# Placing the low parts of H by time in a routed expert kernel: set times, four H banks, a refitted placing model

## The chip, the cores and the metric

The kernel runs on one core of a Trainium2 chip. The metric is the device time of one execution in microseconds (us); smaller is better. The engines are PE (matrix products, with a queue of weight loads beside it), DVE (vector arithmetic), ACT (activations and copies), POOL (here it issues the gathers and scatters) and SP (plain DMA issues).

## The reference, cut to what matters

A batch of 8 sequences (512 local and 32 global tokens, 8 heads of 64) goes through windowed attention; its output is x, N = 8 x 544 = 4352 tokens by 512. Then E = 8 experts, each with room for N // E = 544 tokens, are filled greedily from the largest gate value down:

```python
cap = N // E
logits = x @ w_gate
order = np.argsort(-logits.flatten())
for idx in order:                      # largest first
    tok, e = idx // E, idx % E
    if assigned[tok] >= 0 or counts[e] >= cap: continue
    assigned[tok] = e; counts[e] += 1
for e in range(E):
    mask = assigned == e
    h = np.maximum(x[mask] @ w1[e], 0.0)   # 512 -> 1024
    out[mask] = h @ w2[e]                  # 1024 -> 512
```

## The kernel before

The attention fills the first part of the span (to about 240 us); the change does not touch it. Then `experts` runs eight experts one after the other, numbered from 0 here. Beside each expert's products, the *routing* finds the tokens of the next one: eight search steps (matmuls `r_oh,r_G` and `r_ce,big` on PE, a scan and comparisons on DVE), then which expert was filled (`vs`, `widx`: which weights to gather), a prefix sum (`r_cs`), one-hot tables (`r_ohh`, `rhs`, four pieces `r_ohl`), the matmuls `r_ohl,rhs` and `c,r_w` on PE, and from these the token list `idx`, by which POOL gathers x.

An expert's products are made in fp32r with a high and a low part of each operand, so that three products (high-high, high-low, low-high) stand for one in full precision:

- *H stage*: 16 blocks H, each 128 rows of h by 272 tokens, 12 matmuls a block (line 876 before). ACT writes the high part `hh` as Relu of the PSUM bank, DVE then the low part `hl` = max(H, 0) - hh; after that the bank is free.
- a small product for the last 32 tokens (line 893), in full precision out of `h32`.
- *Y stage*: four tiles Y of 128 tokens by 512, 24 matmuls each (line 903); ACT copies each to `y`, POOL scatters it to the output. "Y40" is the place behind the 40th of these 96 matmuls.

Between them lie, for the *next* expert: the gather of its W1 (`w1r`, two of 1 MB) and W2 (`w2r`), the split of both into high (ACT, `w1h`, `w2h`) and low parts (DVE, `w1l`, `w2l`), the gather of its x (`xg`, five tiles), their transposes on PE into H banks (line 741), and the split into `xh` (ACT) and `xl` (DVE).

All instructions of an engine run in the order in which the program was written, and this order is set by a placing model while the program is built. `V.now` is the model's time on PE: each matmul adds a constant (`step`). `V.busy` is when DVE would be through with all it has been given: each operation adds a fixed charge and a charge per element (`Queue`). Work for later is kept in a list `todo` with a time and a condition; `step` starts at most one such piece per matmul when its time has come. Where the condition has `calm()`, DVE must be less than AHEAD = 200 ns behind. The routing is a generator: it yields the model time from which it may go on (`ready`: DVE's end + 400 ns; `pace`: DVE's end - 250 ns). Before, it yields -1 where an `hl` may go in: `bubble` then issues what is in `fill`. `bubble` is also called when DVE would be idle, and at the end of a block all that is in `fill` is issued ahead of adding the new one. At an expert's end a loop lets the model's time run on, with no matmul, until the next expert's gathers, W1's first half and the transposes have been placed:

```python
while nxt < E and (pending(f"g{nxt}", f"h{nxt}", f"a{nxt}", f"x{nxt}", f"v{nxt}") or nxt not in raw1):
    step(120)
    bubble()
```

PSUM's eight banks are H 3, Y 3 and two for the routing (R, R2).

Of the kernel before, what the change touches and what calls it, by code (L numbers as in the profile page):

```python
# [8 lines left out]
F32 = mybir.dt.float32  # L9
# [4 lines left out]
ALU = mybir.AluOpType  # L14
# [4 lines left out]
B, H, SL, SG, D = 8, 8, 512, 32, 64  # L19
S = SL + SG  # L20
DM = H * D
# [351 lines left out]
HOP = 400  # L373
SLACK = 100
PACE = 250
CU = 64
LAND = 1000
CF = 1024
# [4 lines left out]
class Queue:  # L383
# [12 lines left out]
    def __getattr__(s, name):  # L396
        op = getattr(s.eng, name)

        def issue(*args, **kw):
            aps = [x for x in list(args) + list(kw.values()) if hasattr(x, "dtype") and hasattr(x, "shape")]  # L400
            n = max(int(np.prod(x.shape[1:])) for x in aps)
            fast = name in ("tensor_scalar", "tensor_copy") or name == "tensor_tensor" and all(
                mybir.dt.size(x.dtype) == 2 for x in aps)
            s.busy = max(s.busy, s.now) + 130 + n * (2.2 if "scan" in name else 0.55 if fast else 1.05)
            return op(*args, **kw)  # L405
        return issue


class Routing:
# [103 lines left out]
    def search(s):  # L513
        nc = s.nc
        for it in range(NIT):
            yield -1
            yield s.when
            A = s.ps.tile([128, 2, E], F32, name="R")
            for i in range(18):
                j, r = slice(2 * i, 2 * i + 2), 32 * (i % 4)  # L520
                g, o = (s.G[:, j].rearrange("p a b -> p (a b)"), s.oh[:, j]) if i < 17 else (s.one, s.rem)
                s.mm(A[r:r + 32], g, o, ns=20, start=(i < 4), stop=(i >= 14))
            p = s.ps.tile([128, 16, E], F32, name="R2")
            if it == 0:
                lo = s.t("lo", [34], I32)
                lof = s.t("lof", [34])
                s.V.tensor_scalar(lo, s.u, 0xffff, None, op0=ALU.bitwise_and)
                s.V.tensor_scalar(lof, lo, 2.0 ** -16, None, op0=ALU.mult)
                s.x = s.hi
            else:  # L530
                x = s.t("x%d" % (it % 2), [34])
                if it == 3:
                    s.V.scalar_tensor_tensor(x, s.x, P, lof, op0=ALU.subtract, op1=ALU.add)
                else:
                    s.V.tensor_scalar(x, s.x, P, None, op0=ALU.subtract)
                s.x = x
            ce = s.t("ce", [2, 16, E], F16)
            s.V.tensor_tensor(ce, A[:, :, None, :].to_broadcast([128, 2, 16, E]),
                              s.dk[:, :, :, None].to_broadcast([128, 2, 16, E]), op=ALU.mult)
            when = s.V.ready()  # L540
            yield -1
            yield when
            for k in range(2):
                s.mm(p, s.big, ce[:, k], start=(k == 0), stop=(k == 1))
            pm = s.t("pm%d" % (it % 2), [16 * E])
            s.V.tensor_tensor_scan(pm, p.rearrange("p a b -> p (a b)"), s.fin[:, it], 0.0, op0=ALU.max,
                                         op1=ALU.min)
            P = pm[:, 16 * E - 1:16 * E]
            if it < NIT - 1:
                s.cand(s.x, P, it + 1)  # L550
        s.P = P.bitcast(I32)

    def phase(s, ph):
# [16 lines left out]
        a = s.t("a", [34])  # L570
# [18 lines left out]
        p = s.ps.tile([128, 68], F32, name="R")  # L589
# [4 lines left out]
        if more:  # L594
            g = s.t("gt", [34], BF16)
# [12 lines left out]
        hl = s.t("hl", [2, 34], I32)  # L608
# [10 lines left out]
        rhs = s.rhs  # L619
# [3 lines left out]
        ohl = s.t("ohl", [64, 34], BF16)  # L623
        for k in range(4):
            q = slice(16 * k, 16 * k + 16)
# [10 lines left out]
        p = s.ps.tile([128, 64], F32, name="R2")  # L636
        for j in range(34):
            r = 32 * (j % 4)
            s.mm(p[r:r + 32], rhs[:, :, :, j].rearrange("p a b -> p (a b)"), ohl[:, :, j], ns=20, start=(j < 4),
                 stop=(j >= 30))  # L640
        if not last:
            s.V.scalar_tensor_tensor(s.act, s.wt, vs, s.act, op0=ALU.not_equal, op1=ALU.mult)
        if more:
# [3 lines left out]
                                     op1=ALU.min)  # L647
# [8 lines left out]
        p = s.ps.tile([128, 6], F32, name="R2")  # L656
# [26 lines left out]
def experts(ctx, tc, A, xd, ident, rt, out):  # L683
# [3 lines left out]
    ps = ctx.enter_context(tc.tile_pool(name="fps", bufs=1, space=PSUM))  # L687
# [7 lines left out]
    hh = wp.tile([128, 8, CAP], F32R, name="hh")  # L695
    hl = wp.tile([128, 8, CAP], F32R, name="hl")
    h32 = wp.tile([128, 8, 32], F32, name="h32")
    sizes = [128, 128, 128, 128, 32]
    HF = CAP // 2
# [36 lines left out]

    def trans_x(xg, t):
        n = sizes[t]
        p = ps.tile([128, 4, 128], F32, name="H", bufs=3)
        for d in range(4):  # L740
            nc.tensor.transpose(p[:, d, :n], xg[t][:n, 128 * d:128 * d + 128], ident[:n, :n])  # L741
        q = slice(128 * t, 128 * t + n)
        nc.scalar.activation(xh[:, :, q], p[:, :, :n], AF.Copy)
        V.tensor_tensor(xl[:, :, q], p[:, :, :n], xh[:, :, q], op=ALU.subtract)
# [12 lines left out]
    V = rt.V  # L757
    V.now = V.busy = 0.0
    pool, dma, need = [0.0], [0.0], [0.0]
    fill, todo, raw1 = [], [], {}  # L760
# [17 lines left out]

    routing = chain()

    def bubble():
        while fill:
            fill.pop(0)()

    def at(tag, t, f, cond=None):
        todo.append((tag, t, cond, f))
# [8 lines left out]

    def step(ns):
        V.now += ns
        for i, (tag, t, cond, f) in enumerate(todo):
            if t <= V.now and (cond is None or cond()):
                todo.pop(i)  # L800
                f()
                break
        while not done[0] and V.now >= need[0]:
            v = next(routing, None)
            if v is None:
                done[0] = True
            elif v < 0:
                bubble()
            else:
                need[0] = v  # L810
        if V.busy < V.now and (done[0] or need[0] > V.now + SLACK):
            bubble()

    def low1(p, j):
        split_w1(raw1[p], j, V)
# [40 lines left out]
    def ffn(ph):  # L856
        nxt = ph + 1
        t0 = V.now
        cur[0] = ph
        half = []  # L860
        if nxt < E:
            at(f"g{nxt}", t0, lambda: get_w1(nxt, half), lambda: nxt in rt.widx and not pending(f"b{ph}"))
            at(f"h{nxt}", t0, lambda: get_x(nxt), lambda: nxt in rt.idx and (mid[0] == ph or V.now > t0 + TX))
            at(f"v{nxt}", t0, lambda: get_w2(nxt), lambda: mid[0] == ph and nxt in rt.widx and
               (not pending(f"h{nxt}") or V.now > t0 + TW))
        for f in range(8):
            if f == 4:
                force(f"b{ph}")
                half.append(True)
            for hf in range(2):  # L870
                q = slice(HF * hf, HF * hf + HF)
                p = ps.tile([128, HF], F32, name="H", bufs=3)
                fs = slice(128 * f, 128 * f + 128)
                for d in range(4):
                    for k, (w, x) in enumerate(((w1h, xh), (w1h, xl), (w1l, xh))):
                        nc.tensor.matmul(p, w[d][:, fs], x[:, d, q], start=(d + k == 0), stop=(d + k == 5))  # L876
                        step(117)
                nc.scalar.activation(hh[:, f, q], p, AF.Relu)  # L878
                if hf:
                    nc.scalar.activation(h32[:, f], p[:, HF - 32:HF], AF.Relu)  # L880
                while fill:
                    fill.pop(0)()
                fill.append(lambda p=p, f=f, q=q: V.scalar_tensor_tensor(
                    hl[:, f, q], p, 0.0, hh[:, f, q], op0=ALU.max, op1=ALU.subtract))

        while fill:
            fill.pop(0)()
        force(f"w{ph}")

        p = ps.tile([128, 128], F32, name="Y", bufs=3)  # L890
        for f in range(8):
            for c in range(4):
                nc.tensor.matmul(p[32 * c:32 * c + 32], h32[:, f], w2r[f // 4][:, f % 4, 128 * c:128 * c + 128],  # L893
                                 start=(f == 0), stop=(f == 7))
            step(220)
        mid[0] = ph
        out_tile(ph, 4, p)
        for t in range(4):
            p = ps.tile([128, DM], F32, name="Y", bufs=3)
            for f in range(8):  # L900
                q = slice(128 * t, 128 * t + 128)
                for k, (h, w) in enumerate(((hh, w2h), (hh, w2l), (hl, w2h))):
                    nc.tensor.matmul(p, h[:, f, q], w[f], start=(f + k == 0), stop=(f + k == 9))  # L903
                    step(216)
            out_tile(ph, t, p)
        while nxt < E and (pending(f"g{nxt}", f"h{nxt}", f"a{nxt}", f"x{nxt}", f"v{nxt}") or nxt not in raw1):
            step(120)
            bubble()

    raws = None  # L910
    for _ in rt.setup(slice(28, 34)):
        pass
    heat = ps.tile([128, HF], F32, name="H", bufs=3)
    for _ in rt.phase(0):
        if raws is None and 0 in rt.widx:
            raws = load_w1(0)
# [96 lines left out]
```

## Time and profile before

| | |
|---|---|
| median of 3 runs | 752.21 us (750.55 to 753.65) |
| profiled execution | 749.67 us |
| its span, first to last instruction | 747.9 us |
| mean granted PE clock | 0.963 |
| PE busy | 694.7 us (93%) |
| DVE busy | 503.1 us (67%) |
| ACT busy | 307.0 us (41%) |
| POOL busy | 159.7 us (21%) |
| DMA moved | 120.56 MB |

In the rows of the profile, "L876 PE MATMUL H<-xh,w1h" is an instruction of line 876 on PE that writes H out of xh and w1h. A row of the timeline has the start, the duration, the engine, the line, the instruction, how many were merged (x4) and in brackets the idle time of its engine before it and what ended that. All DVE instructions of the routing and of the placing model have the line of the helper that issues them (405), so they are told apart by their tiles.

### The profile page before, as it was taken

What the parts mean: (1) busy time and instruction counts of PE and PEld (TensorE: products, weight loads), DVE (VectorE), ACT (ScalarE), POOL (GpSimd) and SP (SyncE); (2) the same over time, 40 slices, a digit from 0 to 9 for tenths busy, and PEclk for the clock granted to TensorE, in tenths of its full rate; (3) what the DMA queues carried; (4) which work ended last, traced back from release to release, by engine and by line L of the source; (5) the groups of instructions that cost most, each with busy time, mean ns of one, the idle gap of its engine ahead of it and who ended that gap; (6) DMA issues with size and microseconds to landing.
All of it is one profiled execution on the core that took longest, in us unless ns stands there. A gap on an engine that the chain in (4) does not pass through costs nothing. (4 is left out here: it accounts for less than half of the span.)

```text
span 747.9 us, 21853 instructions
## 1 busy us (share of the span) xinstructions
PE 694.7 (93%) x9012; PEld 568.2 (76%) x9012; DVE 503.1 (67%) x1855; ACT 307.0 (41%) x841; POOL 159.7 (21%) x190
## 2 busy tenths in 40 slices
PE   7989999999997269999999999999999999999993
PEld 6666777777774149878878977987987987988982
DVE  5787887877867787777777777776776763641300
ACT  4655666666662033234324324333333432543310
POOL 5221122111100040051051142132023034311011
PEclk9999999999998558999999999999999999999997
DMA  9997888988721061081080054144045046431000
GB/s 348 409 375 267 319 314 280 318 309 302 290 72 60 2 212 74 2 301 44 6 313 29 13 168 154 27 166 158 13 146 171 30 146 211 163 117 57 2 32 28
DMA packets 32419, 120.56 MB, mean 161 GB/s; under 512 B 6720, under 2 KB 6976, under 8 KB 24128
## 3 DMA queue, kind: packets, MB, share of 16 engines
q1 hardware_dynamic: 22080, 67.78, 24.6%
q0 software_dynamic: 10240, 51.39, 19.8%
q8 instruction: 71, 1.16, 0.6%
q14 instruction: 28, 0.23, 0.1%
HBM read 101.32 MB, written 17.83 MB: 159 GB/s over the span
## 5 line engine op out<-in xcount | busy, mean ns | idle before, releaser
L876 PE MATMUL H<-xh,w1h 128*128 128x272 f32 x512 | 152.7, 298 | 2.9 <-DVE hl L405 2.7
L876 PE MATMUL H<-xl,w1h 128*128 128x272 f32 x512 | 151.2, 295 | 0.0
L876 PE MATMUL H<-xh,w1l 128*128 128x272 f32 x512 | 150.4, 294 | 0.0
L145 ACT ACTIVATE p<-p,nm 128x128 f32<-128x128 f32 x256 | 81.7, 392 | 67.7 <-DVE ls L165 34.7
L903 PE MATMUL Y<-w2h,hh 128*128 128x512 f32 x256 | 104.2, 407 | 0.0
L878 ACT ACTIVATE hh<-H 128x272 fp32r<-128x272 f32 x128 | 50.9, 398 | 129.4 <-PE H L876 114.0
L903 PE MATMUL Y<-w2l,hh 128*128 128x512 f32 x256 | 103.6, 405 | 0.0
L876 PEld LDWEIGHTS H<-xh,w1h 128*128 128x128 f32 x512 | 97.6, 191 | 6.7 <-DVE hl L405 3.2
L903 PE MATMUL Y<-w2h,hl 128*128 128x512 f32 x256 | 102.6, 401 | 0.0
L876 PEld LDWEIGHTS H<-xl,w1h 128*128 128x128 f32 x512 | 97.5, 191 | 0.6
L876 PEld LDWEIGHTS H<-xh,w1l 128*128 128x128 f32 x512 | 97.6, 191 | 0.2
L134 PE MATMUL S<-qk,qz 128*64 128x128 f32 x1024 | 70.8, 279 | 5.9 <-DVE qz L86 3.0
L86 POOL COPY qz<-q 64x544 f32<-64x544 f32 x60 | 38.4, 640 | 150.1 <-DMA q<-in_qk_dram 102.0
L405 DVE SCALAR_TENSOR_TENSOR hl<-H,hh 128x272 fp32r<-128x272 f32 x128 | 54.3, 434 | 23.8 <-ACT h L880 13.0
L405 DVE TENSOR_TENSOR w2l<-w2r,w2h 128x512 fp32r<-128x512 f32 x64 | 43.0, 687 | 40.1 <-ACT w2h L718 39.9
L134 PEld LDWEIGHTS S<-qk,qz 128*64 128x64 f32 x1024 | 55.0, 136 | 18.8 <-issue 15.2
L849 ACT ACTIVATE y<-Y 128x512 f32<-128x512 f32 x32 | 19.2, 599 | 119.2 <-PE Y L903 93.3
L141 DVE CUSTOM_DVE_ANT_0 p<-S,mask 128x128 f32<-128x128 f32 x256 | 58.7, 285 | 6.9 <-DMA mask<-in_mask_dram 3.0
L702 POOL DMA_INDIRECT w1r<-in_w_dram,widx x16 | 15.6, 976 | 206.3 <-DVE r_a L405 100.5
L754 POOL DMA_INDIRECT out_dram<-y,idx x32 | 33.0, 1032 | 118.7 <-ACT y L849 45.3
L903 PEld LDWEIGHTS Y<-w2h,hh 128*128 128x128 f32 x256 | 48.1, 188 | 11.5 <-issue 2.2
L903 PEld LDWEIGHTS Y<-w2h,hl 128*128 128x128 f32 x256 | 48.2, 188 | 9.9 <-issue 0.2
(166 smaller groups left out, 1196.8 us busy)
## 6 DMA issues: line engine op xcount, KB each, us to landing
vw<-in_vw_dram SPq DMA_DIRECT2D x32, 1040.0 KB, 8.2
qk<-in_qk_dram SPq DMA_DIRECT2D x32, 432.0 KB, 5.3
q<-in_qk_dram SPq DMA_DIRECT2D x32, 272.0 KB, 6.2
xd<-xs SPq DMA_DIRECT2D x8, 1024.0 KB, 7.1
xd<-xg SPq DMA_DIRECT2D x64, 8.0 KB, 5.6
xg<-xd,idx POOLq DMA_INDIRECT x40, 3.6
mask<-in_mask_dram SPq DMA_DIRECT2D x1, 512.0 KB, 6.2
cf<-in_cf_dram SPq DMA_DIRECT2D x1, 512.0 KB, 12.4
```

The lines of the kernel that those rows point to most:

```text
L86: eng.tensor_copy(z[r, :, h, :], q[r].rearrange("p (j i) -> p j i", i=32))
L134: nc.tensor.matmul(st[64 * r:64 * r + 64, c, :], z[:, j].rearrange("p h i -> p (h i)"), kw[:, k0:k0 + 128], start=True, stop=True)
L141: nc.vector.tensor_tensor_reduce(s.p[:, c, :], st[:, c, :], mask[:, 4 * s.u + c, :], 1.0, -BIG, ALU.add, ALU.max, nm[:, c:c + 1])
L145: nc.scalar.activation(s.p[:, c, :], s.p[:, c, :], AF.Exp, bias=nm[:, c:c + 1], scale=SCALE)
L405: return op(*args, **kw)
L702: nc.gpsimd.indirect_dma_start(out=dst, out_offset=None, in_=src, element_offset=off, in_offset=bass.IndirectOffsetOnAxis(ap=idx, axis=0))
L754: nc.gpsimd.indirect_dma_start(out=out, out_offset=bass.IndirectOffsetOnAxis(ap=rt.idx[ph][:n, t:t + 1], axis=0), in_=y[:n], in_offset=None)
L849: nc.scalar.activation(y[:n], p[:n], AF.Copy)
L876: nc.tensor.matmul(p, w[d][:, fs], x[:, d, q], start=(d + k == 0), stop=(d + k == 5))
L878: nc.scalar.activation(hh[:, f, q], p, AF.Relu)
L903: nc.tensor.matmul(p, h[:, f, q], w[f], start=(f + k == 0), stop=(f + k == 9))
```

## The change

- `hl` gets a time: it is put into `fill` with `V.now + RELU` (700 ns after the block's last matmul), and `low` issues it as soon as the model's time is there, at the start of `step`, ahead of `todo` and of the routing. `bubble` is gone, and the yields of -1 have no effect.
- H has four PSUM banks, Y two.
- The model's constants: a DVE operation is charged 180 ns (130 before) + 0.5 per element for the fast kinds (0.55), 1.9 for a scan (2.2), 1.05 for the others; an H matmul 125 ns (117), a Y matmul 232 (216), a routing matmul 22 (20).

```diff
+RELU = 700
...
-            s.busy = max(s.busy, s.now) + 130 + n * (2.2 if "scan" in name else 0.55 if fast else 1.05)
+            s.busy = max(s.busy, s.now) + 180 + n * (1.9 if "scan" in name else 0.5 if fast else 1.05)
...
-                s.mm(A[r:r + 32], g, o, ns=20, start=(i < 4), stop=(i >= 14))
+                s.mm(A[r:r + 32], g, o, ns=22, start=(i < 4), stop=(i >= 14))
...
-        p = ps.tile([128, 4, 128], F32, name="H", bufs=3)
+        p = ps.tile([128, 4, 128], F32, name="H", bufs=4)
...
-    def bubble():
-        while fill:
-            fill.pop(0)()
+    def low(all=False):
+        while fill and (all or fill[0][0] <= V.now):
+            fill.pop(0)[1]()
...
     def step(ns):
         V.now += ns
+        low()
...
-            elif v < 0:
-                bubble()
-            else:
+            elif v >= 0:
                 need[0] = v
-        if V.busy < V.now and (done[0] or need[0] > V.now + SLACK):
-            bubble()
...
-                        step(117)
+                        step(125)
...
-                while fill:
-                    fill.pop(0)()
-                fill.append(lambda p=p, f=f, q=q: V.scalar_tensor_tensor(
-                    hl[:, f, q], p, 0.0, hh[:, f, q], op0=ALU.max, op1=ALU.subtract))
+                low(len(fill) > 1)
+                fill.append((V.now + RELU, lambda p=p, f=f, q=q: V.scalar_tensor_tensor(
+                    hl[:, f, q], p, 0.0, hh[:, f, q], op0=ALU.max, op1=ALU.subtract)))
...
-            p = ps.tile([128, DM], F32, name="Y", bufs=3)
+            p = ps.tile([128, DM], F32, name="Y", bufs=2)
...
-                    step(216)
+                    step(232)
...
             step(120)
-            bubble()
```

How this moves the program is seen in the order of the instructions. On PE, at the Y stage of expert 3, the transposes of the next expert's x (`H<-ident,xg`, four matmuls a tile) stood after Y40 and Y45, with more Y matmuls behind (this is before):

```order
L903 MATMUL Y<-w2l_4841,hh 128x512
L903 MATMUL Y<-w2h_4833,hl 128x512
L903 MATMUL Y<-w2h_4834,hh 128x512
L741 MATMUL H<-ident,xg 128x128 x4
L903 MATMUL Y<-w2l_4842,hh 128x512
L903 MATMUL Y<-w2h_4834,hl 128x512
L903 MATMUL Y<-w2h_4835,hh 128x512
L903 MATMUL Y<-w2l_4843,hh 128x512
L903 MATMUL Y<-w2h_4835,hl 128x512
L741 MATMUL H<-ident,xg 128x128 x4
L903 MATMUL Y<-w2h_4836,hh 128x512
L903 MATMUL Y<-w2l_4844,hh 128x512
```

The other three tiles followed in the same way, and 39 Y matmuls came after the last. The same transposes in the changed program, where the last row is the next expert's first H matmul:

```order
L899 MATMUL Y<-w2h_4834,hl 128x512
L742 MATMUL H<-ident,xg 128x128 x4
L899 MATMUL Y<-w2h_4835,hh 128x512
L899 MATMUL Y<-w2l_4843,hh 128x512
L899 MATMUL Y<-w2h_4835,hl 128x512
L899 MATMUL Y<-w2h_4836,hh 128x512
L742 MATMUL H<-ident,xg 128x128 x4
L899 MATMUL Y<-w2l_4844,hh 128x512
L899 MATMUL Y<-w2h_4836,hl 128x512
L742 MATMUL H<-ident,xg 128x128 x8
L742 MATMUL H<-ident,xg 128x32 x4
L874 MATMUL H<-xh,w1h_4821 128x272
```

They moved to Y90, Y94 and behind the last Y matmul; the last three tiles stand in one piece ahead of the next expert.

On DVE, in the routing beside the Y stage of expert 2 (`rhs` and `r_ohl` are the one-hot tables, `r_gt` and what follows prepare the next search), before:

```order
L405 TENSOR_TENSOR r_ohh<-r_hb,tab 128x306
L405 TENSOR_TENSOR rhs<-r_ohh,ids 128x306 x2
L405 TENSOR_TENSOR r_ohl<-r_hb,tab 128x544 x4
L405 TENSOR_SCALAR r_gt<-r_st 128x34
L405 TENSOR_TENSOR r_ohg<-r_oh,r_gt 128x272
```

and in the changed program:

```order
L406 TENSOR_TENSOR r_ohh<-r_hb,tab 128x306
L406 TENSOR_TENSOR rhs<-r_ohh,ids 128x306 x2
L406 TENSOR_TENSOR w1l_4825<-w1r,w1h_4821 128x512
L406 TENSOR_TENSOR r_ohl<-r_hb,tab 128x544
L406 TENSOR_TENSOR w1l_4826<-w1r,w1h_4822 128x512
L406 TENSOR_TENSOR r_ohl<-r_hb,tab 128x544
L406 TENSOR_TENSOR w1l_4825<-w1r,w1h_4821 128x512
L406 TENSOR_TENSOR r_ohl<-r_hb,tab 128x544
L406 TENSOR_TENSOR w1l_4827<-w1r,w1h_4823 128x512
L406 TENSOR_TENSOR r_ohl<-r_hb,tab 128x544
L406 TENSOR_SCALAR r_gt<-r_st 128x34
```

Four low parts of the next expert's W1 now lie between the four pieces; w1l_4825 and w1l_4826 come out of the first W1 gather, w1l_4827 out of the second.

More of the change, by code (lines that the diff above doesn't have):

```diff
@@ L638, in phase @@
             r = 32 * (j % 4)
-            s.mm(p[r:r + 32], rhs[:, :, :, j].rearrange("p a b -> p (a b)"), ohl[:, :, j], ns=20, start=(j < 4),
+            s.mm(p[r:r + 32], rhs[:, :, :, j].rearrange("p a b -> p (a b)"), ohl[:, :, j], ns=22, start=(j < 4),
                  stop=(j >= 30))
@@ L871, in ffn @@
                 q = slice(HF * hf, HF * hf + HF)
-                p = ps.tile([128, HF], F32, name="H", bufs=3)
+                p = ps.tile([128, HF], F32, name="H", bufs=4)
                 fs = slice(128 * f, 128 * f + 128)
@@ L880, in ffn @@
                     nc.scalar.activation(h32[:, f], p[:, HF - 32:HF], AF.Relu)
-                while fill:
-                    fill.pop(0)()
-                fill.append(lambda p=p, f=f, q=q: V.scalar_tensor_tensor(
-                    hl[:, f, q], p, 0.0, hh[:, f, q], op0=ALU.max, op1=ALU.subtract))
-        while fill:
-            fill.pop(0)()
+                low(len(fill) > 1)
+                fill.append((V.now + RELU, lambda p=p, f=f, q=q: V.scalar_tensor_tensor(
+                    hl[:, f, q], p, 0.0, hh[:, f, q], op0=ALU.max, op1=ALU.subtract)))
+        low(True)
         force(f"w{ph}")
-        p = ps.tile([128, 128], F32, name="Y", bufs=3)
+        p = ps.tile([128, 128], F32, name="Y", bufs=2)
         for f in range(8):
@@ L912, in experts @@
         pass
-    heat = ps.tile([128, HF], F32, name="H", bufs=3)
+    heat = ps.tile([128, HF], F32, name="H", bufs=4)
     for _ in rt.phase(0):
```

## The prediction

> **What bounds the kernel now.** I read the page first, then TensorE's waits from 300 us on, then the stretches, then single stretches of the timeline. Experts are counted from 0.
>
> ```profile
> PE 694.7 (93%) x9012; PEld 568.2 (76%) x9012; DVE 503.1 (67%) x1855; ACT 307.0 (41%) x841; POOL 159.7 (21%) x190
> L405 DVE SCALAR_TENSOR_TENSOR hl<-H,hh 128x272 fp32r<-128x272 f32 x128 | 54.3, 434 | 23.8 <-ACT h L880 13.0
> ```
> ```profile
> PE H L876 <- DVE hl L405: 2.7, 9, 0.6
> PE R L472 <- DVE r_G L405: 0.9, 3, 0.4
> PE H L741 <- DMA xg<-xd,idx: 0.6, 1, 0.6
> PE R L472 <- DVE r_ce L405: 0.2, 1, 0.2
> ```
> ```profile
> core 0: us, PE busy (x) PEld busy (x) DVE busy (x) ACT busy (x) POOL busy (x), PEclk, DMA share, GB/s
> 40.00:240.00 200.00, 193.01 (x3966) 141.45 (x3968) 157.34 (x833) 120.50 (x376) 30.72 (x48) 0.99 0.74 267
> ...
> 279.00:285.00 6.00, 6.00 (x44) 5.55 (x44) 4.25 (x10) 2.03 (x5) 0.00 (x0) 0.50 0.82 328
> 286.00:294.00 8.00, 8.00 (x95) 7.45 (x94) 6.57 (x15) 4.48 (x13) 0.00 (x0) 1.00 0.00 0
> 294.00:748.00 454.00, 437.25 (x4049) 374.55 (x4047) 277.51 (x754) 154.58 (x376) 104.47 (x103) 0.99 0.30 103
> ```
>
> PE is the bound of the experts: all its recorded waits from 300 us on are 2.7 + 0.9 + 0.6 + 0.2 = 4.4 us. Nine waits for the low part hl are 2.7 us of them. So the change can win 4.4 us at most; whatever else it moves can only cost. DVE works 277.5 of the last 454 us, and its 23.8 us of waiting ahead of hl cost nothing by themselves.
>
> PE's pace, and one of the nine waits:
>
> ```profile
> 326.38 0.39 PE L903 MATMUL Y<-w2h,hl 128*128 128x512 f32 x1
> ...
> 332.41 0.39 PE L903 MATMUL Y<-w2l,hh 128*128 128x512 f32 x1
> 332.64 0.60 PE L741 MATMUL H<-ident,xg 128*128 128x128 f32 x4
> 332.99 0.48 PE L903 MATMUL Y<-w2h,hl 128*128 128x512 f32 x1
> ...
> 344.12 0.29 PE L876 MATMUL H<-xh,w1l 128*128 128x272 f32 x1
> ...
> 345.63 0.28 PE L876 MATMUL H<-xh,w1l 128*128 128x272 f32 x1
> 346.56 0.40 PE L876 MATMUL H<-xh,w1h 128*128 128x272 f32 x1 [0.64 <-DVE hl L405]
> ```
>
> Starts are what counts, since busy times overlap. From 326.38 to 332.41 lie 26 steps: 0.232 us per Y matmul. From 344.12 to 345.63 lie 12 steps: 0.126 us per H matmul, 1.51 us per block. Four transposes of one x tile delay the next Y matmul by 0.35 us (332.64 to 332.99).
>
> **The change, part by part.** *The banks and the set time.* A fourth H bank lets a block start when the block four back is split, 1.51 us more room; the longest of the nine waits is 0.64 us, so I take all 2.7 us as won. The first-come place of hl on DVE can make DVE wait for the Relu instead; that is the 23.8 us above, off the path as long as the routing's pieces reach PE in time. *Y with two banks* costs nothing: a Y tile takes 24 x 0.232 = 5.57 us, and the copy that frees its bank 0.60 (the y row below), so it is due some 5 us before it is missed. If ACT were held that long, PE would wait by the excess.
>
> *The constants and the lost bubble* reorder the program, and this is where the time goes. The constants charge more for most DVE operations and more for each matmul. I counted Y matmuls in the new order. The index matmul "c,r_w" of experts 0 to 5 stood after Y matmul 46, 37, 26, 21, 24 and 13 (13 is expert 5's first one); now it stands after 66, 72, 71, 71, 71 and 69, of 96. x is gathered only after it. The five transposes that stood after Y40 to Y57 in expert 3 stand after Y90, Y94, and three after Y96, with nothing behind them but the next expert's H blocks, which need that x. Today 10 to 47 Y matmuls lie behind the last transposes of experts 0 to 5; this cover goes. What a gather takes from the index matmul on, in expert 3:
>
> ```profile
> 496.11 0.20 PE L472 MATMUL R<-c,r_w 128*128 128x5 bf16 x2
> ```
> ```profile
> 496.78 0.98 POOL L702 DMA_INDIRECT xg<-xd,idx  x1 [5.37 <-DVE r_cl L405]
> 498.07 0.95 POOL L702 DMA_INDIRECT xg<-xd,idx  x1 [0.30 <-issue]
> 499.32 1.43 POOL L702 DMA_INDIRECT xg<-xd,idx  x1 [0.30 <-issue]
> 501.06 0.95 POOL L702 DMA_INDIRECT xg<-xd,idx  x1 [0.30 <-issue]
> 502.31 0.87 POOL L702 DMA_INDIRECT xg<-xd,idx  x1 [0.30 <-issue]
> ```
> ```profile
> DMA to landing us min/median/max: 3.6/3.6/3.6
> ```
> ```profile
> DMA to landing us min/median/max: 2.8/3.2/3.6
> ```
> ```profile
> DMA to landing us min/median/max: 2.8/3.2/3.6
> ```
>
> The first landing row is of the fourth gather alone, the second of the fourth and fifth. Tile 4 is there 501.06 + 3.6 - 496.11 = 8.55 us after the index matmul, tile 5 502.31 + 2.8 - 496.11 = 9.0. PE comes earlier: from Y71 25 matmuls are 5.80, two transposed tiles 0.70, the index group itself 0.1 (an estimate: half a Y matmul), the third tile 0.35: 6.95 us. It waits 1.6 us for tile 4 and, after 0.35 of work, 0.1 for tile 5: 1.7 us each in experts 2, 3, 4. Expert 1 (24 matmuls) gets 1.9; expert 5 (27, with two more routing matmuls) 1.15; expert 0 (30, three tiles before the end) 0.55. **Term A: 0.55 + 1.9 + 3 x 1.7 + 1.15 = 8.7 us.** From below, with all gathers 1.26 us apart as most are, tile 4 comes at 8.05: 0.5 less each, 5.9. From above, a w1l split that now stands ahead of r_cl could hold the gathers, 0.64 us each (below): 12.5. I take 8.7, since the five rows are this very chain.
>
> *W1's low parts between the one-hot pieces.* The gather of W1 starts after the last search step, which now stands at Y7 to Y13 (before: end of H or early Y). Four w1l splits now lie between the four r_ohl pieces in experts 0 to 5, the fourth out of the second W1 gather. Before, expert 4 had three of them there:
>
> ```profile
> 539.01 0.29 PE L472 MATMUL R<-r_ce,big 128*128 128x128 f16 x2
> ...
> 552.12 1.28 PE L472 MATMUL R<-r_ohl,rhs 128*32 128x64 bf16 x34
> ```
> ```profile
> 540.65 0.98 POOL L702 DMA_INDIRECT w1r<-in_w_dram,widx  x1 [17.87 <-DVE r_a L405]
> 541.94 0.96 POOL L702 DMA_INDIRECT w1r<-in_w_dram,widx  x1 [0.31 <-issue]
> ```
> ```profile
> DMA to landing us min/median/max: 5.5/6.5/7.4
> ```
> ```profile
> 546.95 0.69 DVE L405 TENSOR_TENSOR w1l<-w1r,w1h 128x512 fp32r<-128x512 f32 x1 [1.30 <-ACT w1h L718]
> ...
> 550.35 0.69 DVE L405 TENSOR_TENSOR w1l<-w1r,w1h 128x512 fp32r<-128x512 f32 x1
> 550.96 0.44 DVE L405 TENSOR_TENSOR r_ohl<-r_hb,tab 128x544 bf16<-128x544 bf16 x1
> ```
>
> The last piece ended 12.4 us after the search's last matmul (539.01 to 551.40), and r_ohl's matmuls stood at 13.1, after it. In the new order they stand 50 Y matmuls after it: 11.6 us, with the routing groups between some 11.8. The second W1 gather lands at 541.94 + 7.4 - 539.01 = 10.3; ACT's w1h takes 0.6, w1l 0.64 and r_ohl 0.36 as the rows follow each other, with hops 0.4: 12.3 to 12.5. **Term B: 12.5 - 11.8 = 0.7 us in each of six experts, 4.2 us.** From below 0 (if the landing is as the 5.5 of the first gather); from above 1.9 each, 11, if landings are 1.2 us later. I take 0.7, nearest to the one chain shown.
>
> *The first blocks after the wait.* Today xh and xl are made under Y matmuls:
>
> ```profile
> 438.07 0.60 ACT L849 ACTIVATE y<-Y 128x512 f32<-128x512 f32 x1 [4.41 <-PE Y L903]
> ...
> 444.38 0.60 ACT L743 ACTIVATE xh<-H 128x512 fp32r<-128x512 f32 x1 [4.16 <-PE H L741]
> ```
> ```profile
> 445.02 0.69 DVE L405 TENSOR_TENSOR xl<-H,xh 128x512 fp32r<-128x512 f32 x1 [1.66 <-ACT xh L743]
> ```
>
> Now tile 4 is transposed at 8.55 to 9.15, copied until 9.8 and split until 10.5; two small routing operations and tile 5's xl (about 0.7 together) end at 11.2. The second block asks for it 9.25 + 1.51 + 0.13 = 10.9 us after the index matmul. **Term C: 0.3 us six times, 1.8**; bounds 0 and 0.7 each, 4.2.
>
> **Term D, the gain:** 2.7 for hl and 0.6 for the one wait on xg, which Term A now counts anew: -3.3; bounds -4.4 (all waits) and 0 (new ones of the same size).
>
> The sum: 8.7 + 4.2 + 1.8 - 3.3 = +11.4 us. On the profiled execution's 749.67 us (747.9 of span and 1.8 around it) that gives 761.1; it lies 2.5 us under the median of the runs, 752.21, so against the median I say 763.6. 0.5% (3.8 us) is what a measurement here tells from no change: slower means over 756.0.
>
> **Rivals.** *The covers hold and only the waits go.* If POOL issued the gathers 0.9 us apart, tile 5 would land before PE comes, A, B and C would shrink to nothing, and D alone would give 752.2 - 4.4 = 747.8: faster. It decides from A + B + C under 0.6 us on. Against it: no two gathers above start closer than 1.25 us. Chance 0.04.
>
> *Half of it.* Gathers evenly 1.26 us apart, W1 landing earlier, C covered: 5.9 - 4.4 = +1.5, 753.7, no change that can be told. For it: B and C are differences of long chains. Chance 0.10.
>
> *The queues bite harder.* r_cl and the gathers behind a w1l in experts 1 to 5, W1 landing late since W2's gather follows it at once: A 12.5, B 8, C 3, D -2: +21.5, 773.7. Chance 0.10.
>
> *hl is no sooner.* If DVE reaches hl as late as now and four banks don't cover it, 2.7 us come back: 766.3, within the forecast's own range. Chance 0.04.
>
> *The clock falls after each wait.* In the stretch 279 to 285 us PE ran dense matmuls at a granted clock of 0.50, so 6 us at half rate cost 3 us; six times, 18 us: 781.6. Against it stands a gap of 1.63 us in the attention, in a stretch at 0.99:
>
> ```profile
> 45.68 0.66 PE L134 MATMUL S<-qk,qz 128*64 128x128 f32 x8 [1.63 <-issue]
> ```
>
> The waits of Term A are 1.9 us at most, next to that gap. Chance 0.04. [...]
>
> **Numbers.** The forecast itself (A, B and C near their values) has 0.68. Its own range, with B from 0 to 8 and C from 0 to 3, is 757.6 to 768.6. For 8 in 10 I go down to the second rival's 753.5 and up to 771, which leaves out the first, third and fifth rival, 0.18. Slower by over 0.5%: 0.68 + 0.10 + 0.04 + 0.04 = 0.86; same 0.10; faster 0.04.
>
> **What would show it.** TensorE's waits: hl under 0.5 us (four banks right); H by xg about 8 to 9 us in 6 to 10 waits, around the ends of experts 0 to 5 (Term A); R by r_ohl about 4 us in 6 waits (B); H by xl under 2 us (C); no wait of Y for ACT's y. The granted clock after 294 us stays 0.99. I am wrong if the transposes at an expert's end don't wait, if the gathers start sooner after the index matmul than 0.67 us or closer together, or if the routing's searches, which keep their spacing of about 2.4 blocks, wait for DVE often.

## The result, and the profile after

The changed kernel takes **759.24 us** (median of 6 runs, 756.92 to 760.69), the kernel before 751.68 us beside it (6 runs, 750.55 to 753.65): ratio 1.0094, 95% interval 1.0072 to 1.0117. It is 7.6 us slower where 11.4 were forecast, and inside the forecast's range. The profiled execution takes 759.57 us with a span of 757.8, 9.9 us longer than the span before.

TensorE's waits from 300 us on, in the profile of the changed kernel (what was waited for; us in total, times, longest):

```profile
PE H L874 <- ACT xh L744: 4.3, 1, 4.3
PE H L742 <- DMA xg<-xd,idx: 3.2, 4, 0.9
PE R L473 <- DVE r_ohl L406: 2.7, 5, 1.0
PE R L473 <- DVE r_ce L406: 1.2, 4, 0.3
PE R L473 <- DVE r_G L406: 1.0, 4, 0.3
PE H L742 <- issue: 0.4, 2, 0.2
```

They are 12.8 us against 4.4 before. The waits for hl are gone, those for xg have grown, those for r_ohl have come, and the largest is one that the prediction did not have: 4.3 us for xh. The stretch of the experts, then two pieces around that wait (busy us and instructions of PE, its weight loads, DVE, ACT, POOL; granted clock; DMA):

```profile
294.00:758.00 464.00, 437.51 (x4015) 374.48 (x4013) 278.52 (x751) 154.37 (x375) 104.70 (x103) 0.98 0.28 101
637.26:640.67 3.41, 0.61 (x7) 0.33 (x5) 0.22 (x1) 0.00 (x0) 2.55 (x3) 1.00 0.71 241
640.67:647.50 6.83, 5.21 (x23) 4.66 (x24) 3.33 (x8) 2.67 (x6) 0.00 (x0) 0.50 0.66 256
```

PE worked 0.61 us in 3.41, and then the granted clock was 0.50 for 6.83 us. H matmuls start 0.227 us apart in it (643.50 to 647.13, 16 steps) and 0.126 behind it (649.04 to 649.92, 7 steps), so the 5.2 us of matmuls that ran in it lost some 2.3 us, an estimate from these steps. The place in the timeline, at the end of expert 5:

```profile
636.06 0.60 PE L742 MATMUL H<-ident,xg 128*128 128x128 f32 x4
636.85 1.02 PE L742 MATMUL H<-ident,xg 128*128 128x128 f32 x8 [0.20 <-issue]
636.88 0.97 POOL L703 DMA_INDIRECT w1r<-in_w_dram,widx  x1 [0.30 <-issue]
638.16 0.94 POOL L703 DMA_INDIRECT w1r<-in_w_dram,widx  x1 [0.30 <-issue]
641.50 0.60 ACT L744 ACTIVATE xh<-H 128x512 fp32r<-128x512 f32 x1 [5.09 <-remote]
642.16 0.60 PE L874 MATMUL H<-xh,w1h 128*128 128x272 f32 x1 [4.29 <-ACT xh L744]
```

The first row is the third tile's four transposes, the second those of the fourth and fifth tile. ACT, idle for 5.09 us, starts to copy the third tile only at 641.50, 4.8 us after its transposes ended (636.06 + 0.60), and the next expert's first H block needs this tile. "Remote" means that no instruction in the profile ended just before the signal which released ACT. Meanwhile the two gathers of W1 for expert 7 are under way; the first was issued at 636.88, 0.2 us after the third tile's signal was due.

An ordinary end, that of expert 2 (timeline of PE, from the last Y matmul to the next expert's first H matmul):

```profile
455.24 0.40 PE L899 MATMUL Y<-w2h,hl 128*128 128x512 f32 x1
455.71 0.66 PE L742 MATMUL H<-ident,xg 128*128 128x128 f32 x4
457.26 1.12 PE L742 MATMUL H<-ident,xg 128*128 128x128 f32 x8 [0.90 <-DMA xg<-xd,idx]
458.31 0.40 PE L874 MATMUL H<-xh,w1h 128*128 128x272 f32 x1
```

The row records a wait of 0.90 us. By the starts more is lost: from 455.24 to 458.31 are 3.07 us, and the work in it is a Y step of 0.23, two tiles of 0.35 and the small fifth one of 0.36 to 0.55, together 1.3 to 1.5. So 1.6 to 1.8 us are lost. The idle time of a row counts from the end of the matmul before it, which lies up to 0.4 us behind its start, while in a run without waits the next one starts after 0.13 to 0.23; and short waits are not listed at all. From last Y to first H the six ends take 1.52, 3.11, 3.07, 2.96, 3.11 and 6.34 us.

**Where the time went.** "Stretch" is from the first H matmul of expert 0 to the last matmul of expert 7; it leaves out what happens ahead of the experts. Before, it runs from 279.21 to 735.52, 456.3 us; after, from 277.71 to 745.45, 467.7. Of the 11.4 us between them, 7.3 to 8.4 are lost at the six ends without the late xh (20.1 us, less 7.4 to 8.5 of work and 4.3 for xh), 4.3 are that wait, 2.3 the half clock behind it, 2.7 and 1.1 more waits for r_ohl and for r_ce with r_G; hl (some 5 us, see e2) and the old xg wait give most of the rest back, and 1 to 2 us of it are not located. The first H matmul came 1.5 us earlier, which makes it the 9.9 of the span.

### The profile page after: what moved, and what is told of

It is laid out like the page before. It is cut to its first block, busy times and chain, and to the rows that moved or that the text cites. A ratio compares the mean times of both kernels' runs of the same rounds, so it can differ in the third digit from the quotient of the medians.

```text
span 757.8 us, 21849 instructions
## 1 busy us (share of the span) xinstructions
PE 695.0 (92%) x9012; PEld 569.1 (75%) x9012; DVE 505.8 (67%) x1855; ACT 306.9 (40%) x841; POOL 159.9 (21%) x190
## 3 DMA queue, kind: packets, MB, share of 16 engines
q8 instruction: 71, 1.16, 0.6%
## 5 line engine op out<-in xcount | busy, mean ns | idle before, releaser
L874 PE MATMUL H<-xh,w1l 128*128 128x272 f32 x512 | 152.4, 298 | 0.0
L899 PE MATMUL Y<-w2l,hh 128*128 128x512 f32 x256 | 102.0, 398 | 0.0
L406 DVE TENSOR_TENSOR w2l<-w2r,w2h 128x512 fp32r<-128x512 f32 x64 | 43.9, 690 | 48.4 <-ACT w2h L719 47.9
L406 DVE SCALAR_TENSOR_TENSOR hl<-H,hh 128x272 fp32r<-128x272 f32 x128 | 54.5, 435 | 20.3 <-ACT h L878 10.7
L719 ACT ACTIVATE w1h<-w1r 128x512 fp32r<-128x512 f32 x64 | 36.9, 624 | 55.7 <-DVE r_c L406 29.8
L406 DVE TENSOR_TENSOR w1l<-w1r,w1h 128x512 fp32r<-128x512 f32 x60 | 40.9, 686 | 26.5 <-ACT w1h L719 24.6
L899 PEld LDWEIGHTS Y<-w2h,hh 128*128 128x128 f32 x256 | 48.1, 188 | 11.4 <-issue 2.0
```

What stands on the lines that cost most here:

```text
L719: nc.scalar.activation(hi, raw, AF.Copy)
```

## The experiments

All of them in one table; "waits" are PE's in the experts, from the profile, and "half clock" is the time at a granted clock of 0.50 after 290 us and before the program's last matmuls.

| run | what it is | median us | ratio to before, 95% | stretch | waits | half clock |
|---|---|---|---|---|---|---|
| before | | 751.2 to 752.4 | | 456.3 | 4.4 | 0 |
| after | the change | 759.24 | 1.0072 to 1.0117 | 467.7 | 12.8 | 6.8 |
| e1 | after, again | 758.20 | 1.0061 to 1.0121 | 467.2 | 11.4 | 6.8 |
| e2 | before + banks 4 and 2 | 743.95 | 0.9855 to 0.9925 | 452.7 | 3.9 | 0 |
| e3 | before + constants | 761.73 | 1.0080 to 1.0159 | 470.2 | 11.9 | 6.8 |
| e4 | after, old charge of DVE | 759.43 | 1.0062 to 1.0136 | 467.5 | 12.2 | 3.4 |
| e5 | after, all constants old | 750.57 | 0.9956 to 1.0015 | 457.4 | 5.2 | 3.4 |
| e6 | before + constants + banks | 757.04 | 1.0043 to 1.0082 | 465.0 | 8.7 | 10.2 |
| e7 | after, old steps of PE | 783.89 | 1.0383 to 1.0449 | 492.1 | 22.7 | 44.4 |
| e8 | after, r_ohl in one piece | 747.27 | 0.9917 to 0.9956 | 454.6 | 2.3 | 0 |
| e9 | before, again (one run) | 748.02 | | 458.8 | 8.0 | 0 |
| e10 | e5 with 128 more PE instructions | 761.24 | 1.0065 to 1.0127 | 466.8 | 10.8 | 10.2 |
| e11 | after, expert 7's W1 later | 756.02 | 1.0026 to 1.0091 | 462.9 | 10.1 | 0 |
| e12 | e2 with r_ohl in one piece | **742.63** | 0.9821 to 0.9891 | 450.9 | 2.8 | 0 |

**e1, the changed kernel once more.**

> The changed kernel once more. Theory 1 (late index: waits for x at the ends of experts 0 to 5 and for the one-hot pieces, out of the new placing): 757 to 761 us, TensorE's waits for xg 3 to 4 us and for r_ohl 2.5 to 3 us again. Rival (the single 4.3 us wait for xh at the end of expert 5 and the half clock behind it are the larger part of the loss): if the wait is a chance event it is gone from this profile, and this execution is 6 to 8 us shorter than the last profiled one, 750 to 753; if it belongs to the program it stands at the same place with about the same length.

Its TensorE waits:

```profile
PE H L742 <- DMA xg<-xd,idx: 3.8, 6, 0.9
PE R L473 <- DVE r_ohl L406: 2.1, 4, 1.1
PE H L874 <- ACT xh L744: 1.8, 1, 1.8
PE H L874 <- DVE xl L406: 1.1, 3, 0.6
```

758.20 us, as theory 1 has it, with r_ohl a little under its 2.5. The same waits in other sizes: xh 1.8 instead of 4.3 at the same place, xg 3.8, xl 1.1. The rival gets neither a wait that is gone nor one of the same length. What moves from one execution to the next is the late signal and the clock, not the waits for xg and r_ohl.

**e2, the banks alone.**

```diff
-        p = ps.tile([128, 4, 128], F32, name="H", bufs=3)
+        p = ps.tile([128, 4, 128], F32, name="H", bufs=4)
...
-            p = ps.tile([128, DM], F32, name="Y", bufs=3)
+            p = ps.tile([128, DM], F32, name="Y", bufs=2)
```

> The kernel before with four H banks and two Y banks and nothing else; the order of all instructions is that of before. Theory 1: the nine waits for hl go, 2 to 3 us less than before, 748.5 to 750, and no wait of Y on ACT's copy. Rival (hl is late because DVE reaches it late, whatever the banks): waits for hl stay above 1.5 us and the time is that of before within 1 us.

743.95 us: 7.3 us faster, more than theory 1 gave it and more than the 2.7 us that the profile of before lists for hl. The order of instructions is that of before; waits for hl are 0.4, and none is for Y's banks. Part of the rest is what such a row does not count. One wait for hl in the last expert, in the profile of before:

```profile
691.09 0.29 PE L876 MATMUL H<-xl,w1h 128*128 128x272 f32 x1
691.22 0.28 PE L876 MATMUL H<-xh,w1l 128*128 128x272 f32 x1
691.77 0.39 PE L876 MATMUL H<-xh,w1h 128*128 128x272 f32 x1 [0.27 <-DVE hl L405]
692.00 0.29 PE L876 MATMUL H<-xl,w1h 128*128 128x272 f32 x1
```

The row says 0.27 us. The starts say 0.55 + 0.23 where two steps are 0.13 each: 0.53 us lost, since the idle time counts from the end of a matmul, 0.28 us behind its start where a step is 0.13, and the first step after the wait is 0.10 us longer than the others. Expert 7, which has no routing beside it, takes 48.69 us with three banks (48.71 in e9, 48.65 in e3) and 48.16 with four, in every run of the table that has four. With as much beyond the record for each (0.26 us), the nine waits cost 2.7 + 2.3 = 5.0 us, an estimate from this one. In the stretch e2 gains 3.6 against the first profile of before and 6.1 against the second (e9).

**e3, the constants alone.**

```diff
-            s.busy = max(s.busy, s.now) + 130 + n * (2.2 if "scan" in name else 0.55 if fast else 1.05)
+            s.busy = max(s.busy, s.now) + 180 + n * (1.9 if "scan" in name else 0.5 if fast else 1.05)
...
-                    step(216)
+                    step(232)
```

(with the H step 125 and the routing matmul 22, as in the change)

> The kernel before with the new constants alone: three H banks, three Y banks, hl issued in the bubbles as before. In the order its index matmuls stand after Y61, Y70, Y71, Y71, Y71, Y69 and the last transposes behind Y96, nearly as in the changed kernel. Theory 1 (the constants make the loss): 757 to 763 us, with waits for xg of 2.5 to 4 us and for r_ohl of 2 to 3 us. Rival (hl at a set time ahead of all else holds the routing and makes the loss): 750 to 753 us.

761.73 us, 10.5 us slower: the constants make all of the loss, and more. TensorE's waits in e3:

```profile
PE H L741 <- DMA xg<-xd,idx: 3.0, 4, 1.0
PE H L876 <- DVE xl L405: 2.6, 1, 2.6
PE H L876 <- DVE hl L405: 2.4, 8, 0.7
PE R L472 <- DVE r_ohl L405: 1.8, 3, 0.8
```

The waits for xg and r_ohl of the changed kernel are there without its banks and its set time, and hl's are back. The single 2.6 us for xl are something else: they stand at the end of expert 5, where ACT starts to copy the third tile 2.6 us after its transposes ended (642.51 against 639.93), so this is the late signal again.

**e4, the old charge of DVE in the changed kernel** (130, 2.2, 0.55; the new steps of PE stay).

> The changed kernel with the old charge for DVE operations (130 ns, 0.55, 2.2), all else as changed. The index matmuls stand after Y37, Y23, Y5 of experts 0 to 2 and in the H stage from expert 3 on, with at least 25 Y matmuls behind the last transposes. Theory 1: no wait for xg at an expert's end, none for r_ohl, none for hl: 746 to 749.5 us, faster than both kernels. Rival (the routing's pieces reach TensorE too early when DVE is charged too little): waits of R for r_G, r_ce, r_x and r_ohl grow to 4 us or more and the time is 750 to 756.

759.43 us: theory 1 fell. With the old charge and the slower steps the model has DVE through sooner, and puts the routing forward: the index matmul of expert 2 stands at Y5, those of experts 3 and 4 in the H stage. The gathers are then no problem (xg 0.2 us), and TensorE waits for routing tiles instead:

```profile
PE Y L889 <- issue: 3.8, 8, 1.0
PE R L473 <- DVE r_ohl L406: 3.3, 3, 2.0
PE R L473 <- DVE r_ce L406: 2.2, 5, 0.6
PE R L473 <- DVE r_oh L406: 1.1, 1, 1.1
PE R L473 <- DVE r_mo L406: 1.1, 1, 1.1
```

The rival's mechanism, 7.7 us of waits for r_ohl, r_ce, r_oh and r_mo, is there, in a larger size than it was given; the time lies above both ranges. The 3.8 us of "issue" inside the small Y products have no releaser that the trace shows.

**e5, all constants old** (the banks and the set time are left).

> The changed kernel with the old charges and steps: banks 4 and 2 and the set time of the low part alone. Theory 1 (the set time is worth nothing on the path, the constants make the whole loss): like the kernel with banks alone, 743.95 us; between 741 and 747, xg waits 2 to 4 us, hl waits under 0.4. Rival (hl put ahead of all else on DVE makes routing pieces late, so that the set time costs what lies between constants + banks and the changed kernel): 748 to 756, with waits of TensorE for routing tiles (r_ohl, r_ce, r_G) of 3 us more than with banks alone.

750.57 us, no change against before, and 6.6 us over the banks alone: theory 1 missed. The rival's time came, its sign did not: the waits for r_ohl, r_ce and r_G are 1.5 us against 2.6 in e2, not 3 us more. Most of the loss stands at one place. In e5, at the end of expert 5:

```profile
620.57 1.27 PE L473 MATMUL R<-r_ohl,rhs 128*32 128x64 bf16 x23 [0.21 <-DVE r_ohl L406]
622.92 0.35 PE L473 MATMUL R<-r_ohl,rhs 128*32 128x64 bf16 x4 [1.08 <-issue]
623.64 0.28 PE L473 MATMUL R<-r_ohl,rhs 128*32 128x64 bf16 x1 [0.38 <-issue]
624.36 0.43 PE L473 MATMUL R<-r_ohl,rhs 128*32 128x64 bf16 x6 [0.45 <-issue]
```

34 small matmuls that take 1.3 us elsewhere take 4.2, while the gathers of W2 and x are in flight, and the clock is at half for 3.4 us after them: 1.9 + 1.5 of the 4.7 us by which the stretch is longer than in e2 (the 1.5 is an estimate: at half clock Y matmuls start 0.425 us apart in e10, 636.16 to 637.86, for 0.232).

**e6, constants and banks on the old scheduling** (e2 and e3 together).

> The kernel before with the new charges and steps and with banks 4 and 2, low parts still in bubbles. Theory 1 (the parts add: +10.5 us for the constants, -7.3 us for the banks, against 751.2): 754 to 756, and the set time then accounts for 2 to 4 us of the changed kernel's 758 to 759. Rival (set time nothing): as the changed kernel, 757.5 to 760, hl waits under 0.5 us. In both the xg waits stay at 3 to 5 us in 6 to 8 waits at the ends of experts 0 to 5.

757.04 us, between the two theories. It lies 2 us under the changed kernel, and the intervals meet: what the set time costs on top of the new constants isn't told apart from nothing. The waits for xg are 4.3 us in 8 waits, as both expected, and a late xh (1.9 us) stands at the same place.

**e7, the index matmul later still** (the old steps 117, 216 and 20, with the new charge).

> The changed kernel with the old steps of TensorE and the new DVE charge: the index matmul stands at Y80 to Y88 instead of Y66 to Y72, all five transposes behind the last Y matmul. Theory 1 (the chain from the index matmul to tile 4 sets each expert's end; 11 to 16 Y matmuls at 0.232 us are 2.5 to 3.7 us): xg waits grow from 0.8 to 3.3 to 4.5 us at each of 6 boundaries, +15 to +22 us: 773 to 781. Rival (the gathers are bound by something else than the index matmul, such as POOL's queue): the waits stay at 0.8 to 1.5 us, 757 to 763. If gaps this long halve the granted clock after each boundary, 6 x 1.7 to 3.4 us more than theory 1: 784 to 800.

783.89 us: theory 1 with the falling clock, 0.1 us under the range that this gave. All five transposes now stand behind the Y stage, and TensorE waits for nearly every tile:

```profile
PE H L742 <- DMA xg<-xd,idx: 20.9, 22, 2.2
```

From last Y to first H the six ends now take 47.9 us instead of 20.1; 4.6 of the difference are transposes which moved there, 23 are lost on top. And the clock falls after each of experts 0 to 5, for 3.4 to 10.2 us; the H matmuls in these stretches run 24 us, which by the changed kernel's steps, 0.227 us for 0.126, costs some 11, where that kernel has 2.3. (The routing's waits, 4.9 us in the changed kernel, are 1.1 in return.) These parts add up to 3 or 4 us more than the 24.4 us by which the stretch is longer; that difference is not located. One of the falls, with the 3.4 us ahead of it (columns as above):

```profile
399.10:402.52 3.42, 0.66 (x4) 0.42 (x4) 1.75 (x7) 1.68 (x3) 2.79 (x3) 1.00 0.64 157
402.50:409.30 6.80, 5.79 (x24) 4.59 (x25) 4.41 (x10) 2.08 (x5) 3.65 (x4) 0.50 0.42 125
```

No single wait is longer than 2.2 us; ahead of the falls stand several, with transposes between them.

**e8, the four pieces of r_ohl without a pause.**

```diff
-            if k < 3:
-                yield s.V.pace()
```

> The changed kernel with the four r_ohl pieces issued without a pause between, so that no split of w1l comes between them. Theory 1 (term B: r_ohl's last piece is late behind w1l splits, 0.3 to 1.0 us in five experts): r_ohl waits under 0.7 us instead of 2.1 to 2.7, index matmul 3 to 11 Y matmuls sooner, so xg waits under 2.5 us: 753 to 756. Rival (the pieces together hold DVE 1.5 us and make hl or the splits late in their place): r_ohl waits gone, waits for hl or w1l of 1 to 3 us, 757 to 760.

747.27 us, 11 to 12 us under the changed kernel, far more than theory 1 gave it. All waits that are left:

```profile
PE H L740 <- DMA xg<-xd,idx: 1.2, 2, 0.6
PE R L473 <- DVE r_G L406: 0.5, 3, 0.2
PE H L740 <- issue: 0.2, 1, 0.2
PE R L473 <- DVE r_ce L406: 0.2, 1, 0.2
PE H L872 <- DVE hl L406: 0.2, 1, 0.2
```

12.8 us have become 2.3, and the half clock at 640 us is gone; the stretch is 13.1 us shorter. With the pieces together the index matmul stands at Y57 to Y68 instead of Y66 to Y72, 3 to 12 earlier, so x is gathered 0.7 to 2.8 us sooner, against some 1.7 us lost at an end. From last Y to first H the six ends take 6.8 us instead of 20.1. So the pauses, with the w1l that they let in between the pieces, held up r_ohl and through it all that follows; the run does not tell the w1l's own time from the earlier places that the model gives the index matmul and what hangs on it.

**e9, the kernel before once more.**

> The kernel before, unchanged, for a second profile: its first profile shows 4.4 us of TensorE waits and no fall of the granted clock between 286 us and the end, at 749.67 us, under the median of 751.2 to 752.2. Theory 1 (banks alone gain 7 us over the median because the typical execution of the kernel before also loses to waits at the ends of experts and to clock halvings): this profile is at 751 to 756, with 6 us or more of waits or one to three stretches of half clock after 290 us. Rival (the first profile is typical and the gain of the banks comes from elsewhere): 749 to 751, waits 4 to 5 us, no half clock after 290 us.

748.02 us, lower than either theory, with waits of 8.0 us (r_ce 2.5, hl 2.2, hh 1.4) as theory 1 had them and no half clock as the rival had it. It begins the experts at 275.12 us instead of 279.21 and then needs 458.8 instead of 456.3. Neither is confirmed; single executions of one kernel differ by this much.

**e10, the code moved by half a piece.**

```diff
+    for _ in range(32):
+        nc.tensor.matmul(heat[:, :128], ident, ident, start=True, stop=True)
     for _ in rt.phase(0):
```

> The run with the old charges and steps, the set time and banks 4 and 2 (750.57 us), with 32 more dummy matmuls on ident ahead of the first routing phase, where TensorE waits for DVE: they move every later TensorE instruction by 128 in the program, half of a 16 KB piece of code. Theory 1 (its profile's 2.9 us of issue waits inside runs of 34 r_ohl matmuls, at 472 to 530 and 621.8 to 624.4 us, are TensorE waiting for a piece of its code, whose fetch at 622.92 us stands behind the gathers of W2 and x; with the half clock after it 4.6 us): no issue wait over 0.5 us in r_ohl, 743.5 to 747, and then the set time is worth nothing against banks alone (743.95). Rival (DVE's order with the set time makes the loss): 749 to 752 as without the shift.

761.24 us, above both theories. No single wait inside r_ohl is over 0.5 us, which theory 1 had as its sign, but the run still breaks, at the same place of the program, into five pieces:

```profile
633.03 0.27 PE L473 MATMUL R<-r_ohl,rhs 128*32 128x64 bf16 x1 [0.42 <-issue]
...
635.19 0.45 PE L473 MATMUL R<-r_ohl,rhs 128*32 128x64 bf16 x7 [0.43 <-issue]
```

TensorE's last fetch of code (16 KB each: queue q8 of the changed kernel has 71 packets of instructions, 1.16 MB) was at 621.87 us, 11 us earlier, so a fetch of code isn't the cause of this break. What e5 and e10 have in common here is traffic of gathers and of a store of y, which ends at 625.2 and 635.7 us, where the run of matmuls ends too (624.8 and 635.6).

The larger surprise is the time. 32 dummy products that have nothing to do with the experts make e5's kernel 10.7 us slower. The experts begin 3.6 us later, and the stretch is 9.4 us longer: the waits are 5.6 us more, among them 2.7 us for r_ce, before which DVE had been idle for 4.7 us ("remote", at 512.45), and the clock is at half for 6.8 us more. So what the late signals and the clock make of a program can outweigh the 6.6 us between e5 and e2, and these 6.6 us are not shown to be the set time's.

**e11, expert 7's W1 later.**

```diff
-            at(f"g{nxt}", t0, lambda: get_w1(nxt, half),
+            at(f"g{nxt}", t0 + (8000 if nxt == E - 1 else 0), lambda: get_w1(nxt, half),
```

> The changed kernel with the two gathers of W1 for expert 7 behind the last stores of expert 5, some 12 us later (about 649 instead of 637 us). Theory 1 (at the end of expert 5 the transposes' signal to ACT comes 2 to 4 us late while these gathers are in flight, PE waits for xh 1.8 to 4.3 us and the clock halves for 3.4 to 6.8 us): the wait for xh is under 0.5 us and no half clock after 630 us, 752 to 755.5. Rival (the late signal comes from TensorE or ACT themselves, the transposes behind one another at the end): the wait for xh stays at 1.8 to 4.3 us, 757 to 760.

The profiled execution takes 753.72 us, as theory 1 says, and at the place in question ACT starts on the third tile 1.3 us after its transposes ended instead of 4.8:

```profile
635.15 0.60 PE L742 MATMUL H<-ident,xg 128*128 128x128 f32 x4
637.07 0.60 ACT L744 ACTIVATE xh<-H 128x512 fp32r<-128x512 f32 x1 [2.28 <-PE H L742]
...
642.98 0.98 POOL L703 DMA_INDIRECT w1r<-in_w_dram,widx  x1 [0.30 <-issue]
```

The gather of W1 moved by 6 us (642.98 against 636.88), not by 12. The wait for xh is 0.5 us, and the clock does not fall. The median, 756.02 us, lies between the two theories: five of ten runs are under 756, and the interval overlaps that of the changed kernel. So with the gathers away the signal is less late in this profile. That the gathers are its cause is not shown (see the last section), and neither is a gain of 3 us in the median.

**e12, the best of both:** the old constants, the banks, and r_ohl in one piece.

> The kernel before with banks 4 and 2 and with the four r_ohl pieces without a pause between, old charges and steps. Theory 1 (the index matmul 2 to 22 Y matmuls sooner than with banks alone, so that the xg and routing waits of 5.4 us shrink by half): 740 to 743.5. Rival 1 (those waits lie elsewhere, no change): 743.5 to 745.5. Rival 2 (a run of small matmuls falls on a code piece behind gathers, as in the run with old constants and set time): 746 to 751 with issue waits of 2 us or more.

742.63 us, as theory 1 has it and 1.1 to 1.8% under the kernel before, and 16 us under the changed kernel. It is the fastest here; against the banks alone (743.95) the intervals overlap. Its waits are xg 1.3, r_ce 0.7, r_G 0.6 and r_ohl 0.2, together 2.8 us against 3.9 with the banks alone, so they did not shrink by half; the index matmul stands 0 to 12 Y matmuls sooner, not 2 to 22.

## Why the prediction was right, point by point

- **Direction and cause: right.** The constants make the loss, by placing r_ohl, the index matmul and the transposes later. They cost 10.5 us in the kernel before (e3), 13.1 with the new banks (e2 to e6) and 8.7 with the set time as well (e5 to the changed kernel). One such pair would not be enough, since e10 moved a time as far with dummies alone; three pairs, the waits at the ends and e7 agree. The chance of slower, 0.86, rested on that.
- **Term A (8.7 us): right.** By the starts 7.3 to 8.4 us are lost at the six ends: 0.4 to 0.6 at expert 0, 1.5 to 1.8 at each of 1 to 4, 0.6 to 0.8 at 5 besides the late xh, where 0.55, 1.9, 1.7 three times and 1.15 were forecast. The fourth gather's tile is transposed 8.65 us after the index matmul (448.61 to 457.26 in expert 2) for the 8.55 of the forecast. What the prediction said of the list of waits was wrong: it shows 3.2 us of xg, not 8 to 9, because the term was counted in starts and the list counts from ends. In e7 the index matmul stands 13 to 17 Y matmuls later still, and the same ends lose 23 us more. (A small slip: the lower bound of this term is 5.7 by its own rows, not 5.9.)
- **Term B (4.2 us): about right as a wait, undervalued as a cause.** 2.7 us in five waits (2.1 in e1; 3.1 by the starts) for 0.7 in each of six. But the prediction added A and B as if they were apart. e8 takes B's cause away, and most of A, the late xh and the half clock go too: 13 us of the stretch. What holds up r_ohl holds up the index matmul.
- **Term C (1.8 us): too much.** No wait for xl in the changed kernel's list, 1.1 us in e1.
- **Term D (-3.3 us): too small, the step that failed.** The prediction took 2.7 us for hl from the rows of waits, while it counted its losses in starts. By the starts the nine waits cost about 5 us, and the banks alone take 3.6 to 6.1 us from the stretch and 7.3 from the median (e2). With the new constants, which the changed kernel has, the banks take 4.7 us from the median and 5.2 from the stretch (e3 to e6). "The change can win 4.4 us at most" was wrong.
- **Y with two banks: nothing,** as forecast (no such wait in any run).
- **The set time: open.** Against the banks alone the time is 6.6 us longer with the old constants (e5), most of it at one place where gathers are in flight, but e10 shows that dummies alone can move the time by more; with the new constants it can't be told from nothing (e6).
- **The rival of the falling clock (0.04) was wrong for most ends and right for some.** In the changed kernel one of the six ends had it, some 2.3 us; in e1 two; in e7 six, some 11 us. The prediction took half rate for its stretch of 6 us, 3 us lost; by the steps there, 0.227 us (280.59 to 282.63) for 0.126, it is 2.7. The prediction argued from one gap of 1.63 us in the attention, and looked at the length of single gaps; its sign, a clock that stays at 0.99, came out as 0.98.
- **The other rivals.** "The covers hold" (747.8) and "half of it" (753.7) lie below the 759.24 us, "the queues bite harder" (773.7) above it; "hl is no sooner" is answered by a list without hl.
- **What it lacked:** the late signal to xh and the half clock behind it, 4.3 + 2.3 us in this profile (1.8 us of waiting in e1). B, C and D came out lower than forecast by about as much (1.5, 1.8 and 2.3 or more), so that the sum came near: 11.4 us for 9.9 between the two profiled spans, though only 7.6 between the medians. Part of its nearness is luck. That the late signal lies on the path at all fits the lost cover: signals are late in e9 and e2 too, where Y matmuls behind the transposes hide them (last section).

## What to carry to other kernels

Where a planner's constants set the order, look at what stands behind the last use of a cover: here 10 to 47 Y matmuls behind the transposes hid the gathers, and a few constants, moved by 7 to 38%, took them away. Follow the chain that the late piece feeds, not the piece alone: without the pauses that led to 2.7 us of waits for r_ohl, the stretch was 13 us shorter. And take the cost of a short wait on TensorE from the starts of the matmuls around it, gains and losses alike, since its row can show half (0.27 of 0.53 us in the profile of before).

## What was not expected of the hardware

**The clock.** From 231 us on all changes of the granted clock in the trace of the changed kernel lie whole multiples of 3.413 us apart, and in the experts of all runs a half-clock stretch is one, two or three of them long. Counted on that grid, the piece ahead of a fall had 0.61 us of PE's work (changed kernel, 637.26), 0.66 to 1.59 (e7, six times), and three times some 2.3: 2.25 in e3, 2.27 in e6 and 2.30 in e1:

```profile
518.40:521.81 3.41, 2.30 (x16) 1.41 (x15) 1.95 (x4) 2.34 (x5) 1.74 (x2) 1.00 0.54 173
521.81:525.22 3.41, 3.41 (x17) 3.41 (x17) 1.72 (x5) 0.54 (x2) 0.99 (x1) 0.50 0.20 77
```

The longest wait in that piece was 0.89 us, for xg. A piece of the changed kernel with 2.35 us of work had no fall, but neither had two of e7 with 1.93 and 2.17 and one of e10 with 1.87, so the busy time of a piece alone does not tell whether a fall follows. Nor does the longest wait in the piece: ahead of a fall it was 0.89 us in e1 and up to 2.2 us in e7, while the 0.90 us at the end of expert 2 in the changed kernel had no fall behind it. What decides a fall is not shown.

**Signals of TensorE that come late.** Rows with "remote" as the releaser, behind 1.0 to 5.1 us in which the engine was idle, occur in the changed kernel and in e1, e3, e4, e5, e6 and e10. The other runs have no such row, but that does not mean that all their signals come in time: where some other matmul ended near the signal, the row names that one. It shows in the times. In e9, the second profile of the kernel before, ACT starts to copy the fourth tile that is transposed beside expert 2's Y stage 1.8 us after its transposes ended:

```profile
442.73 0.60 PE L741 MATMUL H<-ident,xg 128*128 128x128 f32 x4
445.09 0.60 ACT L743 ACTIVATE xh<-H 128x512 fp32r<-128x512 f32 x1 [2.73 <-PE H L741]
```

In the first profile the same step takes 0.04 us (448.53 + 0.60 to 449.17). e2, e9 and e12 have several such delays, of 1.0 to 2.3 us, and TensorE waits for xh in none of them, since Y matmuls lie behind the transposes. In the changed kernel the last three tiles have no such cover.

In the cases above, gathers of 1 MB (W1, W2) or of x were in flight. But at the end of expert 5 the third tile's copy is late by 4.8 us in the changed kernel, 2.6 in e1 and e3, and still 1.3 in e11 without the gathers of W1; in e8 the fourth tile's copy is on time there, with the first gather of W1 issued 0.2 us ahead of its transposes. So these gathers alone do not decide it. A fetch of code was ruled out as the cause of the break inside one run of small matmuls (e10). Why signals of TensorE come late in one execution and not in another of the same kernel is open; the trace shows no queue in which they meet the gathers.
